# A recurrence and two feed-forward layers on one core: who issues the first loads and block 0's stores, how many weight sets are fetched early, and when columns are split

## The chip, the core and the metric

The kernel runs on one core of a Trainium2 chip. Its time is the device time of one execution in microseconds, from runs of the same program; the median of three runs of the kernel before is 937.01 us (936.17 to 940.31). The engines' names here: PE is TensorE (PEld its weight loads), DVE is VectorE, ACT is ScalarE, POOL is GpSimd, SP is SyncE.

## The reference

Three stages in a row, all in float32:

```python
# stage 1, per batch (4), head (8) and step t (768), head size 48
y[t]  = r[t] @ (state + outer(u * k[t], v[t]))
state = w[:, None] * state + outer(k[t], v[t])
# stage 2 on x = y as [3072, 384]; w_in is 384 x 2048, w_out 2048 x 384
h = x @ w_in;  x2 = maximum(0.01 * h, h) @ w_out
# stage 3, other weights of the same shapes
h = x2 @ w_in; out = (h * cos(h)) @ w_out
```

## The kernel before

**Stage 1** is cut into 24 units of 128 steps (6 per batch), each in two halves of 64. Within a half the recurrence is matmuls: scores of k and r (tiles pa and pd, L370), a state update (pu, L383 and L388) and the outputs (py, L512 and L516). Between them VectorE scales by powers of w (tile pt): X multiplies k (L354), R multiplies r (L357), Z makes k times u (L360), NK scales the other copy of k (L364); M and N select the triangle (L374). ScalarE moves states (S1 L394, S0 L411) and copies y to yo (L520). Units 0 to 7 use this early form; from unit 8 on an older form is used (prep L433 to L439, pieces L459, L466, L495).

**Columns.** y of a unit is stored to DRAM (L522, by SP for units 0 to 5) and read back transposed as columns xl (L594, by POOL for units 0 to 5). `split_xu` then casts xl to a rounded xh on ScalarE (L598) and subtracts on VectorE (L599). Four units make a block of 512 columns.

**Stages 2 and 3** run over slots (j, f): block j (0 to 5 of stage 2, 6 to 11 of stage 3) and one of 16 weight sets f. g1 of a slot is 9 matmuls (L611), then ScalarE and VectorE make ga, gh and gl (L623, L625, L651, L653), and two slots later g2 adds 9 matmuls (L665 to L667). At f = 15 of a block g2 copies three tiles ob (m = 0 and 2 by ScalarE, m = 1 by VectorE) and stores them (L680). Blocks 0 and 1 come one after the other; the slot number in the text counts g1 from 0, so block 0 is slots 0 to 15, block 1 is 16 to 31, block 2 starts at 32, and g2 of slot 15 stands in slot 17.

**Weights.** A set is 768 KB, loaded by SP (`load_w`, L148, tile raw) and decoded into two parts by `split_w`, which is a generator of four quarters: ACT L314; ACT L316; DVE L318, L319 and ACT L321; DVE L326, L327, L330. Tiles of sets 12 to 15 are lent to units 2 and 3 at first.

**Order.** SP follows the order of the program's text throughout. PE, VectorE and ScalarE follow it up to slot 16 (HAND); after that a scheduler orders them. The opening is: constants, loads of units 0 to 3 and sets 0 to 2, then the decays (pw, pt), an If on a flag (L253; its body is a slow path that is not taken here), the tables, and the list `first`, written out by hand for units 0 to 5 (SOLO), with ("x", n) for the split of unit n's columns, ("d", 0) for one quarter of decoding, ("l", n) for the load of unit n and ("w", f) for set f. After that come the slots; pieces of units 6 and 7 are spread over slots 0 to 15, those of units 8 to 11 over slots 18 to 28. Loads of units 8 and 9 are held and issued with the first piece of unit 8, in slot 18.

**Touched lines.** `load` (L118; unit 1's load is issued by ScalarE, L160), the copy of wi into the last column of pt (L233), the store of ob (L680), and the list `first` (L734 to L753).

```python
    load(0)
    nc.scalar.dma_start(out=ut, in_=uT)
    load(1, nc.scalar)
    load_w(0, 0)
...
        nc.scalar.copy(out=pt[:, 1, :, HC - 1:HC], in_=wi)
...
                (nc.sync if j == nb - 1 else getattr(nc, QO)).dma_start(out=dst, in_=ob)
```

Of the kernel before, what the change touches and what calls it, by code (L numbers as in the profile page):

```python
# [21 lines left out]
HC = C // 2  # L22
# [3 lines left out]
NF = DFF // 128  # L26
# [17 lines left out]
SOLO = 6  # L44
# [7 lines left out]
QO = 'scalar'  # L52
# [8 lines left out]
def moe_rwkv_kernel(ctx: ExitStack, tc, wT, uT, wq, uu, rs, ks, nat, wmoe, out):  # L61
    nc = tc.nc
# [49 lines left out]
    def ring(u):  # L112
        return u if u < UB else u % 2

    def v_of(u):
        return vf_[ring(u)] if u < ONE else vs_[u % 2]

    def load(u, q=nc.sync):  # L118
        src = nat[u * C:(u + 1) * C].rearrange("t i (h d) -> t i h d", h=H)
        if u < ONE:  # L120
            t, n = kf_[ring(u)], None
        else:
            t = ap_.tile([PACK, H, HC], F32, tag="ks", bufs=KSB, name="kst")
            n = ap_.tile([128, 2, H, D], F32, tag="nat", bufs=NATB, name="natt")
        q.dma_start(out=t, in_=ks[u])
        if u < ONE:
            q.dma_start(out=rf_[ring(u)], in_=rs[u])
        else:
            for c in range(2):
                q.dma_start(out=ar_[u % 2][ROWS[c], c], in_=rs[u, ROWS[c]])  # L130
        if u < ONE:
            q.dma_start(out=nk_[ring(u)], in_=src[:, 1])
        else:
            q.dma_start(out=n, in_=src[:, 0:2])
        for c in range(2):
            q.dma_start(out=v_of(u)[TOK[c], c], in_=src[TOK[c], 2])
        U["ks", u], U["nat", u] = t, n
# [7 lines left out]
    def load_w(L, f):  # L145
        pool, i = set_of(L, f)
        t = wraw[L, f] = pool.tile([128, 2, 384, 2], I32, tag=f"w{i}", name=f"raw{i}")
        nc.sync.dma_start(  # L148
            out=t.rearrange("p z a b -> p z (a b)"), in_=wmoe[L, f].bitcast(I32).rearrange("z p c -> p z c"))
# [6 lines left out]
    nc.sync.dma_start(out=wt, in_=wT)  # L156
    ut = const.tile([PACK, H], F32, name="ut")
    load(0)
    nc.scalar.dma_start(out=ut, in_=uT)
    load(1, nc.scalar)  # L160
    load_w(0, 0)
    load(2)
    load_w(0, 1)
    load(3)
# [10 lines left out]
    for i in range(2):  # L175
        nc.gpsimd.affine_select(
            out=mask[TOK[i]], in_=mask[TOK[i]], pattern=[[1, HC]], base=0, channel_multiplier=-1,
# [5 lines left out]
    pt = ap_.tile([PACK, 2, H, HC], F32, name="pt")  # L183
    wi = ap_.tile([PACK, H, 1], F32, name="wi")
# [20 lines left out]
    def stir(n):  # L205
        o = psum.tile([128, DM], F32, tag="h", bufs=2, name="stir")
        for i in range(n):
            nc.tensor.matmul(out=o, lhsT=still[:, 0:128], rhs=still, start=i == 0, stop=i == n - 1)

    def decays():  # L210
        nc.vector.tensor_scalar(out=ws, in0=wt, scalar1=W_LO, scalar2=W_HI, op0=ALU.max, op1=ALU.min)
        ge = const.tile([PACK, H], F32, name="ge")
        cnt = const.tile([PACK, 1], F32, name="cnt")
        flag = const.tile([1, 1], I32, name="flag")
        nc.vector.tensor_tensor(out=ge, in0=ws, in1=wt, op=ALU.is_equal)
        nc.vector.tensor_reduce(out=cnt, in_=ge, axis=AX.X, op=ALU.min)
        stir(1)
        tot = psum.tile([1, 1], F32, tag="a1", name="tot")
        nc.tensor.matmul(out=tot, lhsT=cnt, rhs=ones, start=True, stop=True)
        stir(2)  # L220
        for i in range(H):
            nc.vector.tensor_tensor_scan(
                out=pw[:, i], data0=ws[:, i:i + 1].to_broadcast([PACK, HC]), data1=ones.to_broadcast([PACK, HC]),
                initial=1.0, op0=ALU.mult, op1=ALU.mult)
        nc.vector.tensor_scalar(out=flag, in0=tot, scalar1=PACK - 0.5, scalar2=None, op0=ALU.is_lt)
        nc.vector.reciprocal(out=wi, in_=wc)
        nc.vector.tensor_tensor(out=wi[HALF[0]], in0=wi[HALF[0]], in1=wi[HALF[0]], op=ALU.mult)
        nc.vector.tensor_tensor(out=wd, in0=wc, in1=wc, op=ALU.mult)
        nc.scalar.copy(out=pt[HALF[0], 0, :, 0:1], in_=wc[HALF[0]])
        nc.scalar.copy(out=pt[HALF[1], 0, :, 1:HC], in_=pw[HALF[1], :, 0:HC - 1])  # L230
        nc.vector.tensor_tensor(
            out=pt[:, 1, :, 0:HC - 1], in0=pw[:, :, HC - 2::-1], in1=wi.to_broadcast([PACK, H, HC - 1]), op=ALU.mult)
        nc.scalar.copy(out=pt[:, 1, :, HC - 1:HC], in_=wi)  # L233
        return flag

    def tables():
# [328 lines left out]
    nb = len(blocks)  # L565
# [90 lines left out]
    def g2(slot):  # L656
        j, f = slot
        gh, gl = gs.pop(slot)
        if f == 0:
            op[j] = [psum.tile([128, NB], F32, tag=f"{'a' if j else 'o'}{m}", name=f"po{m}") for m in range(KT)]  # L660
        w_h, w_l = wsel.pop(slot)
        for m in range(KT):
            o = op[j][m]
            sl = slice(m * 128, (m + 1) * 128)
            nc.tensor.matmul(out=o, lhsT=w_l[:, 1, sl], rhs=gh, start=(f == 0), stop=False)  # L665
            nc.tensor.matmul(out=o, lhsT=w_h[:, 1, sl], rhs=gh, start=False, stop=False)  # L666
            nc.tensor.matmul(out=o, lhsT=w_h[:, 1, sl], rhs=gl, start=False, stop=(f == NF - 1))  # L667
        if f == NF - 1:
            L, t0, n = blocks[j]
            for m in range(KT):  # L670
                if j == nb - 1 and m == KT - 1:
                    ob = mp.tile([128, NB], F32, tag="ga", bufs=2, name="ga")
                else:
                    ob = mp.tile([128, NB], F32, tag="ob", bufs=OB2, name="ob")
                if m == 1:
                    nc.vector.tensor_copy(out=ob, in_=op[j][m])
                else:
                    nc.scalar.copy(out=ob, in_=op[j][m])
                dst = (out if L else x2t)[m * 128:(m + 1) * 128, t0:t0 + n]
                (nc.sync if j == nb - 1 else getattr(nc, QO)).dma_start(out=dst, in_=ob)  # L680


    slots = [(0, f) for f in range(LB)]
# [9 lines left out]
    for j in range(1, N1):  # L693
        a = 0 if j == 1 else at[0][1] + LAG + 1 if j == 2 else at[2][0] + PACE * (j - 3)
        b = a + PACE if j > 2 else at[j][0] - 4 if j != 1 else SPREAD
        n = ends[j] - (ends[j - 1] if j > 1 else pieces.index(("p", SOLO)) + 2)
# [27 lines left out]
    def quarter(si=-1):  # L724
        if ready[0] == NF or si in REST:
            return
        if not part:
            part.append(split_w(0, ready[0]))
        if next(part[0], part) is part:
            ready[0] += 1  # L730
            part.clear()

    do = {"w": lambda f: load_w(0, f), "y": piece_y, "l": load, "d": lambda f: quarter(), "x": split_xu}
    first = [("X R Z NK", 1), ("PA PD M N", 0), ("w", 3), ("w", 4), ("w", 5)]  # L734
    for u in range(SOLO):
        x = {2: [("x", 0)], 3: [("x", 1)], 4: [("x", 2)]}.get(u, [])
        q = 3 if u < 2 else 4 if u < SOLO - 1 else 0
        d = [[("d", 0)]] * q + [[]] * 4
        n = u + 1
        first += [("PU S1", u)] + d[0]  # L740
        first += [("PA", n)] if n < SOLO else []
        first += [("PV S0", u)]
        first += [("PD M", n)] if n < SOLO else []
        first += d[1] + x
        first += [("N", n)] if n < SOLO else []
        first += [("X R", u + 2)] if u + 2 < SOLO else []
        first += d[2]
        first += [("Z NK", u + 2)] if u + 2 < SOLO else []
        first += [("y", u)]
        first += {0: [("l", 4), ("w", 6)], 1: [("l", 5), ("w", 7)], 2: [("w", 8)],  # L750
                  4: [("l", 6)], 5: [("l", 7)] + [("w", f) for f in range(9, NF)]}.get(u, [])
        first += d[3]
    first += [("x", 3), ("X R Z NK", SOLO)]  # L753
    flag = decays()
    slow = nc.values_load(flag[0:1, 0:1], min_val=0, max_val=1)
    step_by_step()
# [10 lines left out]
    for si in range(len(slots) + LAG):  # L767
# [34 lines left out]
        if si >= LAG:  # L802
            g2(slots[si - LAG])
# [45 lines left out]
```

## Time and profile before

| what | value |
|---|---|
| median of 3 runs | 937.01 us |
| profiled execution: device time | 936.6 us |
| its span (first to last instruction) | 935.0 us |
| mean granted clock of PE | 0.990 |
| PE busy | 910.1 us (97%) |
| VectorE busy | 634.7 us (68%) |
| ScalarE busy | 542.7 us (58%) |
| chain that ended last | PE 83%, VectorE 5%, ScalarE 2%, DMA 2%, issue 2% |

Busy time of an engine is the union of its instructions; issuing a DMA and waiting don't count. Rows below have start, duration, engine and line, names (out<-in), shape and count; in brackets stands the idle time of the engine before the row and what ended it. All times in rows are counted from the span's start. A q behind an engine's name is its sequencer (waits, branches, DMA issues).

### The profile page before, as it was taken

Reading aid. Unit: us, or ns where it says so; the run is one execution under the profiler, and the core shown is the slowest. Engines: PE = TensorE matmul, PEld = TensorE weight load, DVE = VectorE, ACT = ScalarE, POOL = GpSimd, SP = SyncE. Lnnn points to the kernel's source line nnn. Section 1 sums busy time; section 2 is a strip of 40 time slices with the busy share of each in tenths; the row PEclk is TensorE's granted clock in tenths of the full one; section 3 lists DMA queues with packets and bytes.
Section 4 is the critical chain, followed back from the end, with each engine's and each line's share of the span. In section 5 each row is a group of like instructions: output and inputs, shape, how many; then the busy total and the mean of one; then the engine's idle time right before and its main releaser. Section 6 shows DMA issues by size and latency. Waiting matters only on the chain.

```text
span 935.0 us, 16040 instructions
## 1 busy us (share of the span) xinstructions
PE 910.1 (97%) x6306; PEld 746.6 (80%) x6306; DVE 634.7 (68%) x1047; ACT 542.7 (58%) x1040; POOL 50.4 (5%) x90
## 2 busy tenths in 40 slices
PE   7899998999999999998999999999999999999997
PEld 6777876887888888886888888888888888888885
DVE  5779998675677676656649976665655665665654
ACT  3446766554555555536457776665655665665554
POOL 3010000010110111100000000000000000000000
PEclk7999999999999999999999999999999999999999
DMA  8956024230332422315035420100100101000000
GB/s 250 291 165 234 19 76 124 81 103 24 113 100 65 135 79 71 103 52 186 10 125 169 135 68 1 34 35 1 57 12 1 67 1 34 35 1 0 34 1 34
DMA packets 37790, 73.09 MB, mean 78 GB/s; under 512 B 9392, under 2 KB 14384, under 8 KB 37712
## 3 DMA queue, kind: packets, MB, share of 16 engines
q1 hardware_dynamic: 27888, 49.95, 17.3%
q0 software_dynamic: 4384, 12.59, 4.4%
q10 hardware_dynamic: 5440, 9.51, 2.8%
q8 instruction: 49, 0.80, 0.4%
q14 instruction: 29, 0.24, 0.1%
HBM read 57.88 MB, written 14.16 MB: 77 GB/s over the span
## 4 chain that ended last, share of the span: by engine, by line
PE 83%; DVE 5%; ACT 2%; DMA 2%; issue 2%; SPq 0%; ACTq 0%; DVEq 0%
PE ph L611 39%; PE po L665 13%; PE po L666 13%; PE po L667 13%; PE pa L459 2%; PE py L495 2%; PE pu L466 1%; DVE w L326 1%; DVE gl L653 1%; ACT dt L321 1%; DVE dt L327 1%; DMA natt<-in_nat 1%; DVE dt L318 1%; DMA raw<-in_wmoe 0%; DMA kst<-in_ks 0%
## 5 line engine op out<-in xcount | busy, mean ns | idle before, releaser
L611 PE MATMUL ph<-xh,w 128*128 128x512 f32 x1152 | 301.8, 391 | 1.2 <-DVE w L330 1.2
L611 PEld LDWEIGHTS ph<-xh,w 128*128 128x128 f32 x1152 | 216.8, 188 | 47.5 <-DVE w L330 2.1
L665 PE MATMUL po<-gh,w 128*128 128x512 f32 x576 | 228.4, 397 | 2.0 <-ACT gh L651 2.0
L666 PE MATMUL po<-gh,w 128*128 128x512 f32 x576 | 224.6, 390 | 0.0
L667 PE MATMUL po<-gl,w 128*128 128x512 f32 x576 | 210.7, 390 | 2.2 <-DVE gl L653 2.1
L653 DVE TENSOR_TENSOR gl<-ga,gh 128x512 fp32r<-128x512 f32 x192 | 132.0, 689 | 106.9 <-ACT gh L651 95.1
L651 ACT CAST gh<-ga 128x512 fp32r<-128x512 f32 x192 | 118.8, 619 | 124.5 <-PE po L666 86.5
L611 PE MATMUL ph<-xl,w 128*128 128x512 f32 x576 | 166.5, 393 | 4.8 <-DVE ga L625 2.5
L611 PEld LDWEIGHTS ph<-xl,w 128*128 128x128 f32 x576 | 107.5, 188 | 28.4 <-DVE ga L625 3.1
L665 PEld LDWEIGHTS po<-gh,w 128*128 128x128 f32 x576 | 108.1, 188 | 26.9 <-ACT gh L651 3.3
L667 PEld LDWEIGHTS po<-gl,w 128*128 128x128 f32 x576 | 107.8, 188 | 26.0 <-DVE gl L653 3.5
L666 PEld LDWEIGHTS po<-gh,w 128*128 128x128 f32 x576 | 108.2, 188 | 21.3
L623 ACT ACTIVATE ga<-ph 128x512 f32<-128x512 f32 x96 | 57.0, 594 | 69.7 <-PE ph L611 68.4
L634 DVE SCALAR_TENSOR_TENSOR gt<-gt,ga 128x512 f32<-128x512 f32 x96 | 65.9, 690 | 38.7 <-ACT gt L633 38.3
L639 DVE TENSOR_TENSOR ga<-ph,gt 128x512 f32<-128x512 f32 x96 | 65.8, 688 | 34.2 <-ACT gt L638 33.5
L638 ACT ACTIVATE gt<-gt 128x512 f32<-128x512 f32 x96 | 59.9, 627 | 49.1 <-DVE gt L636 48.9
L625 DVE TENSOR_TENSOR ga<-ph,ga 128x512 f32<-128x512 f32 x96 | 65.7, 686 | 31.7 <-ACT ga L623 31.2
L632 ACT ACTIVATE ga<-ph 128x512 f32<-128x512 f32 x96 | 57.3, 596 | 43.4 <-PE ph L611 28.1
L471 ACT ACTIVATE ar<-ident,bon 64x64 f32<-64x64 f32 x256 | 64.7, 333 | 18.4 <-DVE bon L438 18.1
L633 ACT ACTIVATE gt<-ga 128x512 f32<-128x512 f32 x96 | 60.3, 631 | 2.1 <-ACT ga L632 0.4
L636 DVE TENSOR_SCALAR gt<-gt 128x512 f32<-128x512 f32 x96 | 40.4, 424 | 1.9
L314 ACT COPY dm<-raw 128x768 uint16<-128x768 uint16 x32 | 34.3, 1073 | 10.0 <-DMA raw<-in_wmoe 8.9
(139 smaller groups left out, 752.8 us busy)
## 6 DMA issues: line engine op xcount, KB each, us to landing
raw<-in_wmoe SPq DMA_DIRECT2D x32, 768.0 KB, 6.1
natt<-in_nat SPq DMA_DIRECT2D x16, 384.0 KB, 3.9
kst<-in_ks SPq DMA_DIRECT2D x21, 224.0 KB, 3.3
x2t<-ob ACTq DMA_DIRECT2D x18, 256.0 KB, 2.0
xl<-x2t POOLq DMA_DIRECT2D x6, 768.0 KB, 4.8
xl<-xt POOLq DMA_DIRECT2D x22, 192.0 KB, 3.5
vs<-in_nat SPq DMA_DIRECT2D x42, 96.0 KB, 3.9
out<-ob ACTq DMA_DIRECT2D x15, 256.0 KB, 2.0
```

Of the source, the lines that this page charges most:

```text
L471: nc.scalar.activation(out=ar[q, c, g], in_=ident2[q], func=AF.Copy, scale=bon[q, g:g + 1])
L611: nc.tensor.matmul(out=p, lhsT=w_[:, 0, k * 128:(k + 1) * 128], rhs=x_[:, k], start=(m == 0), stop=(m == 3 * KT - 1))
L625: nc.vector.tensor_tensor(out=ga, in0=p, in1=ga, op=ALU.max)
L633: nc.scalar.activation(out=gt, in_=ga, func=AF.Copy, bias=MAGIC)
L634: nc.vector.scalar_tensor_tensor(out=gt, in0=gt, scalar=MAGIC, in1=ga, op0=ALU.subtract, op1=ALU.subtract)
L638: nc.scalar.activation(out=gt, in_=gt, func=AF.Sin, scale=-TWOPI)
L639: nc.vector.tensor_tensor(out=ga, in0=p, in1=gt, op=ALU.mult)
L651: nc.scalar.copy(out=gh, in_=ga)
L653: nc.vector.tensor_tensor(out=gl, in0=ga, in1=gh.bitcast(F32), op=ALU.subtract)
L665: nc.tensor.matmul(out=o, lhsT=w_l[:, 1, sl], rhs=gh, start=(f == 0), stop=False)
L666: nc.tensor.matmul(out=o, lhsT=w_h[:, 1, sl], rhs=gh, start=False, stop=False)
L667: nc.tensor.matmul(out=o, lhsT=w_h[:, 1, sl], rhs=gl, start=False, stop=(f == NF - 1))
```

## The change

Unit 1's five loads are issued by SP in place of ScalarE. The copy of wi into pt goes from ScalarE to VectorE, ahead of the multiplication that fills the rest of that half of pt. Block 0's three stores go from ScalarE to SP. In `first`, set 3 alone is fetched ahead of unit 0; sets 4, 5 and 6 follow the outputs of units 0, 1 and 2, sets 7 to 15 those of unit 5. The splits of units 0, 1 and 2 move from units 2, 3 and 4 to units 3, 4 and 5, and that of unit 3 from behind the outputs of unit 5 to ahead of them.

```diff
-    def load(u, q=nc.sync):
+    def load(u):
+        q = nc.sync
...
-    load(1, nc.scalar)
+    load(1)
...
         nc.vector.tensor_tensor(out=wd, in0=wc, in1=wc, op=ALU.mult)
+        nc.vector.tensor_copy(out=pt[:, 1, :, HC - 1:HC], in_=wi)
...
         nc.vector.tensor_tensor(
             out=pt[:, 1, :, 0:HC - 1], in0=pw[:, :, HC - 2::-1], in1=wi.to_broadcast([PACK, H, HC - 1]), op=ALU.mult)
-        nc.scalar.copy(out=pt[:, 1, :, HC - 1:HC], in_=wi)
...
-                (nc.sync if j == nb - 1 else getattr(nc, QO)).dma_start(out=dst, in_=ob)
+                (nc.sync if j in (0, nb - 1) else getattr(nc, QO)).dma_start(out=dst, in_=ob)
...
-    first = [("X R Z NK", 1), ("PA PD M N", 0), ("w", 3), ("w", 4), ("w", 5)]
+    first = [("X R Z NK", 1), ("PA PD M N", 0), ("w", 3)]
     for u in range(SOLO):
-        x = {2: [("x", 0)], 3: [("x", 1)], 4: [("x", 2)]}.get(u, [])
+        x = {3: [("x", 0)], 4: [("x", 1)], 5: [("x", 2)]}.get(u, [])
...
+        first += [("x", 3)] if n == SOLO else []
         first += [("y", u)]
-        first += {0: [("l", 4), ("w", 6)], 1: [("l", 5), ("w", 7)], 2: [("w", 8)],
-                  4: [("l", 6)], 5: [("l", 7)] + [("w", f) for f in range(9, NF)]}.get(u, [])
+        first += {0: [("l", 4), ("w", 4)], 1: [("l", 5), ("w", 5)], 2: [("w", 6)],
+                  4: [("l", 6)], 5: [("l", 7)] + [("w", f) for f in range(7, NF)]}.get(u, [])
         first += d[3]
-    first += [("x", 3), ("X R Z NK", SOLO)]
+    first += [("X R Z NK", SOLO)]
```

## Rows read from the trace of the kernel before

**Rows 1.** Busy us by stretch: PE, PEld, DVE, ACT, POOL; granted clock; DMA share; GB/s.

```profile
0.00:63.59 63.59, 51.94 (x1058) 45.39 (x1058) 41.89 (x81) 28.03 (x49) 11.75 (x31) 0.89 0.79 231
...
8.90:19.10 10.20, 10.06 (x147) 9.88 (x148) 6.95 (x12) 3.18 (x12) 0.46 (x1) 0.50 1.05 296
46.40:49.80 3.40, 3.40 (x63) 3.28 (x64) 3.33 (x6) 2.44 (x4) 0.76 (x1) 0.50 0.68 240
```

**Rows 2.** Timeline of PE: tables, y of units 0, 1, 3, 4 (L512), scores, block 0.

```profile
9.04 1.59 PE L242 MATMUL ps_t<-ident,pt 48*64 48x48 f32 x13 [3.08 <-ACT pt L233]
...
21.54 0.33 PE L512 MATMUL py<-ar,vs 128*64 128x64 f32 x4
...
28.45 0.33 PE L512 MATMUL py<-ar,vs 128*64 128x64 f32 x4
...
44.43 1.15 PE L370 MATMUL pa<-ar,kst 48*64 48x64 f32 x32 [3.06 <-DVE ar L357]
...
48.24 0.47 PE L512 MATMUL py<-ar,lent 128*64 128x64 f32 x4
...
55.87 0.33 PE L512 MATMUL py<-ar,vs 128*64 128x64 f32 x4
...
63.59 0.72 PE L611 MATMUL ph<-xl,w 128*128 128x512 f32 x2 [1.72 <-DVE xl L599]
...
65.87 0.51 PE L370 MATMUL pa<-ar,kst 48*64 48x64 f32 x10
```

**Rows 3.** Timeline of ACT: its table load, the copy L233, unit 0's cast.

```profile
6.18 1.28 ACT L201 ACT_TABLE_LOAD   x1 [6.18 <-DMA kst<-in_ks]
...
8.74 0.20 ACT L233 COPY pt<-wi 112x8 f32<-112x8 f32 x1
...
41.46 0.51 ACT L598 CAST xh<-xl 128x384 fp32r<-128x384 f32 x1 [5.55 <-DMA xl<-xt]
```

**Rows 4.** Timeline of DVE: pt, unit 0's k, unit 6's r.

```profile
5.16 0.68 DVE L231 TENSOR_TENSOR pt<-pw,wi 112x504 f32<-112x504 f32 x1
...
8.97 0.69 DVE L354 TENSOR_TENSOR kst<-kst,pt 112x512 f32<-112x512 f32 x1 [3.13 <-ACT pt L233]
...
64.53 0.69 DVE L357 TENSOR_TENSOR ar<-ar,pt 112x512 f32<-112x512 f32 x1
```

**Rows 5.** Timeline of PE: pu (its first half) and pa at either clock.

```profile
15.64 1.27 PE L383 MATMUL pu<-vs,ub 128*48 128x48 f32 x13
...
18.08 1.60 PE L370 MATMUL pa<-ar,kst 48*64 48x64 f32 x32
...
24.05 0.75 PE L383 MATMUL pu<-vs,sm 128*48 128x48 f32 x13
...
25.44 1.15 PE L370 MATMUL pa<-lent,lent 48*64 48x64 f32 x32
```

**Rows 6.** Waits of SP up to 70 us; source L148 from 24.4 to 30.4 us.

```profile
SPq L253 <- SPq L253: 6.2, 1, 6.2
...
L148 SPq DMA_DIRECT2D raw<-in_wmoe x3: 392/453/460, 24.4 to 25.4; - x3
...
DMA to landing us min/median/max: 4.2/5.7/8.9
```

**Rows 7.** Timelines around block 0's end, and unit 11's columns with block 2's start.

```profile
134.23 0.43 SPq L125 DMA_DIRECT2D kst<-in_ks  x1
...
146.22 0.97 PE L667 MATMUL po<-gl,w 128*128 128x512 f32 x3 [1.27 <-DVE gl L653]
...
155.72 0.33 ACTq L680 DMA_DIRECT2D x2t<-ob  x1
...
212.10 0.76 POOL L594 DMA_DIRECT2D xl<-xt  x1 [4.63 <-DMA xt<-yo]
...
225.82 0.84 PE L611 MATMUL ph<-xl,w 128*128 128x512 f32 x3
```

## The prediction

> **What bounds the kernel now.** Over the whole span PE is 97% busy, but not in its first stage: in the 63.59 us ahead of block 0's first matmul PE shows 51.9 us, VectorE 41.9, the DMA engines 0.79 [rows 1]. No engine fills this stage, and the change works there. So look next at what PE waited for: 3.08 us before the table matmuls at 9.04, for ScalarE's copy L233; 3.06 us before unit 4's scores at 44.43, for VectorE; 1.72 us before block 0 at 63.59, for the split of unit 3's columns [rows 2]. Then follow each wait one engine back.
>
> At the start ScalarE computes nothing until 6.18: it issues the loads of unit 1, and only then loads its table and makes its copies, of which L233 ends at 8.94 [rows 3]. VectorE has made the rest of pt by 5.84, then sits idle 3.13 us for that copy [rows 4].
>
> At 41.46 ScalarE had been idle 5.55 us for unit 0's columns coming back from DRAM (line 598) [rows 3]; VectorE's subtraction, and behind it unit 4's multiplications, stood in order behind that cast, and so PE's scores at 44.43. The columns were late because the store of y of unit 0 was. SP stood 6.2 us at the If (L253); then it issued three weight sets, which landed from 4.2 us after the first issue at 24.4 (28.6) to 8.9 us after the last at 25.4 (34.3) [rows 6], and y of unit 0 went out behind them.
>
> After long idleness PE is slow as well: the granted clock is 0.50 (the lower level, 1.2 GHz) from 8.9 to 19.1 and from 46.4 to 49.8 [rows 1], each time behind one of the two 3 us waits.
>
> **The change part by part.**
>
> *Start.* Unit 1's five issues go from ScalarE to SP, and L233 becomes a VectorE copy ahead of L231. ScalarE then has its table and its other two small copies behind it before 6, since L231, which needs the same pw, started at 5.16. L231 ended at 5.84 [rows 4]; the new copy of 112x8 ahead of it I take at 0.2 us, ScalarE's time for the same shape [rows 3]. pt is whole at 6.05, and unit 0's first multiplication starts at about 6.1 in place of 8.97 [rows 4], if its k has landed. Gain 2.85 us. The cost: five issues on SP ahead of set 0 and of the loads of units 2 and 3. Bytes and order on the DMA engines stay nearly the same, and no wait on these loads stands among PE's [rows 2], so I take 0; if that cover is gone, it is at most the gain itself, as the issues then hold SP as long as they held ScalarE.
> The Trainium skill, "DMA: Bandwidth & Descriptors", section "Issuing engines are not separate DMA queues", says that starting DMAs on several engines only saves the sequencer's issue time, which is usually small. By that the first two terms of the sum below fall away (933.1); in the row of 6.18 the issue time is just what is paid.
>
> *Clock at the start.* PE now starts its table matmuls near 6.1, with no 3 us of idleness ahead of them. Nearest rows: both falls came behind 3 us of it [rows 1, 2]. So I take it that the clock stays at 2.4 GHz. What that gives: pu's 32 matmuls took 2.44 us at half (15.64 to 18.08) and 1.39 at full (24.05 to 25.44), a ratio of 1.75; pa's 32 took 1.60 against 1.15, a ratio of 1.39 [rows 5]. Ahead of 15.64 stood two such sets of scores (3.2 us), so PE worked at half from 12.4 to 19.1, 6.7 us. At full that saves 1.9 us (1.39) to 2.9 (1.75). I take 2.4, the middle, as the two forms are mixed. Bounds 0 to 2.9.
>
> *Fewer sets in the first units, splits one unit later.* Sets 4 and 5 leave the place ahead of y of unit 0; from there on each store, load and column transfer meets two sets less. Between 28.6 and 34.3 those two landed, so y of unit 0, the loads of unit 4 and the columns of unit 0 come up to 5.7 us sooner [rows 6]: columns at 41.4 - 5.7 = 35.7. Their split moves from unit 2 to unit 3. Where is unit 3 then? y of units 0 and 1 started at 21.54 and 28.45, a pace of 6.9; a unit with a split in it took from 48.24 to 55.87, 7.6 [rows 2]. With y of unit 0 at 21.54 - 2.85 - 2.4 = 16.3, y of unit 3 comes at 16.3 + 2 x 6.9 + 7.6 = 37.7, and its unit's split about 1 us before that: 36.7 against 35.7. So the 3.06 us go; the margin is 1 us. The loads of unit 4, behind the same store, are as tight. SP's 6.2 us at the If stay: nothing in the change moves them.
> With the wait goes the second low stretch of the clock: 3.4 us at the two ratios, 1.0 to 1.5 us; I take 1.2.
>
> *Split of unit 3 ahead of y of unit 5.* Block 0 no longer waits 1.72 us [rows 2]. But behind its first 9 matmuls come unit 6's scores, at 65.87 [rows 2], and these need VectorE's multiplication of r at 64.53, ended 65.22 [rows 4]. The load for that follows y of unit 4, whose place is unchanged. So only 65.87 - 65.22 = 0.6 us is kept.
>
> *Nine sets in place of seven behind unit 5.* The last set lands by the time of two sets, up to 5.7 us [rows 6], later. It is decoded last, in slot 13, behind 13 slots of some 4 us of matmuls; this hides it. Cost 0.
>
> *Block 0 stored by SP.* ScalarE loses three issues of 0.33 us [rows 7], off the path. But SP keeps the order of the text: the stores of g2 in slot 17 stand ahead of the loads of units 8 and 9, which slot 18 releases. Now load 8 is issued at 134.23, and the third store, by ScalarE, at 155.72 [rows 7]: load 8 can be up to 21.8 us later. Behind SP wait VectorE (prep) and PE (pieces of units 8 to 11). Cover: unit 8 needs the banks that block 0 frees in any case, and unit 11's columns were fetched at 212.10, while block 2 took them at 225.82 [rows 7], 13.7 us, of which I count 10 as slack behind landing and split. On the other side, gl stands behind prep of units 8 and 9 now: PE waited 1.27 us at 146.22 for it [rows 7]. Bounds: 1.3 us of gain to 21.8 of loss. I take 0: from slot 16 on VectorE, ScalarE and PE follow no written order, so prep can be set behind the matmuls at hand.
>
> **Sum.** 2.85 + 2.4 + 3.06 + 1.2 + 0.6 = 10.1. Two hand-overs have 1 us of margin (unit 4's loads, unit 0's columns); I take 1 us off for them: 9.1. The profiled execution took 936.6 (its span 935.0), 0.4 under the median of 937.0. 937.0 - 9.1 = 927.9.
>
> **Rivals.**
> *The clock falls at the start all the same.* Half of the table matmuls wait for ScalarE's eight scalings, and short idle spots stay. For it: the clock stayed low from 8.9 to 19.1 though PE shows 10.06 us busy there [rows 1]. Then 2.4 us are missing: 930.3.
> *The loads hold the units.* The two sets may free less than 5.7 us. If half, columns and loads come 2.8 us later than above, less the margin 1.8, and 1 us more at unit 5: 930.7. For it: the DMA engines' 0.79 [rows 1].
> *The start is worth nothing.* The five issues hold SP in ScalarE's place, unit 0 or 1 waits for its loads, and 5.25 us are missing: 933.1. Against: all these loads share the engines either way. By the rule of the Trainium skill named above ("DMA: Bandwidth & Descriptors") it would come out so.
> *The gain is given back at unit 11.* If load 8's 21.8 us pass on and 10 are slack, PE waits 11.8 us before block 2: 939.7, no change. Against: units 9 to 11 have work of their own between them and can catch up.
> *Slower: SP's stores jam the queue.* If prep of units 8 and 9 keeps its place ahead of gl on VectorE, PE stands for the whole delay, up to 21.8 us: 949.7. It decides from a PE wait of 9.1 us around slots 16 to 18. Against: ob of m = 1 is itself a VectorE copy that must come ahead of these loads, so prep can't stand ahead of all.
>
> **Numbers.** Forecast 0.50; clock 0.16; loads 0.13; start 0.06; given back 0.09; slower 0.06. The likeliest case's own range is 925 to 930. The range's lower end takes 2.85 + 2.9 + 3.06 + 1.5 + 1.72 (all of block 0's wait) + 1.3 (at the preps) = 13.3, or 923.7, and I set it at 922, since loads that come sooner may also shorten waits under 1 us. The upper end, 936, is a start worth nothing together with loads that hold (927.9 + 5.25 + 2.8); it leaves out the last two. Within 0.5% (4.7 us, about what a measurement of this kernel can tell from no change) lie 932.3 to 941.7: given back, start, and a little of the last: 0.14. Slower 0.08, the last rival with more of the kind; faster 0.78.
>
> **What would show it.** ScalarE's table load near 1.4; VectorE's first multiplication near 6.1; granted clock 1.00 from 8.9 to 19.1; no 3 us PE wait before unit 4's scores; block 0 near 53; a small PE wait at unit 6's scores in place of that for unit 3's columns; SP's pause at the If still there. I am wrong if block 0 starts before 56 and the end has not moved with it: then look at load 8, prep of unit 8, PE's gaps from slot 16 on, and the gap before block 2.

## The result: 924.3 us, and the profile after

The kernel after takes 924.31 us (median of 4 runs, 923.51 to 927.92) against 937.03 for the kernel before on the same chip: a ratio of 0.9865, 95% interval 0.983 to 0.990, so 12.7 us less. The forecast was 927.9 with a range of 922 to 936. The profiled execution took 924.3 us, its span is 922.7 against 935.0. Line numbers of the kernel after are one higher than before from L119 on (the multiplication L231 is L233).

The opening, by stretch, as in [rows 1] (PE, PEld, DVE, ACT, POOL; granted clock; DMA share; GB/s). The last row is slots 15 to 31, 90.20 us long before:

```profile
0.00:54.06 54.06, 48.56 (x1058) 41.40 (x1058) 42.11 (x82) 27.70 (x47) 11.43 (x30) 0.97 0.85 236
...
9.73:13.14 3.41, 3.41 (x60) 3.29 (x57) 3.31 (x7) 0.00 (x0) 0.06 (x1) 0.50 1.02 272
...
127.70:213.40 85.70, 85.70 (x704) 69.18 (x704) 61.44 (x102) 49.11 (x141) 7.69 (x12) 1.00 0.33 100
```

Block 0 starts at 54.06 in place of 63.59. In these two executions the low clock (0.50, the level of 1.2 GHz) shrank from 10.2 us to 3.4 us at the start, and the second low stretch is gone. PE in order of time, to be laid beside [rows 2]:

```profile
6.26 0.96 PE L243 MATMUL ps_t<-ident,pt 48*64 48x48 f32 x13
...
17.14 0.68 PE L371 MATMUL pd<-ar,natt 48*64 48x64 f32 x15 [0.89 <-issue]
17.75 0.33 PE L513 MATMUL py<-ar,vs 128*64 128x64 f32 x4
...
24.21 0.27 PE L371 MATMUL pa<-lent,lent 48*64 48x64 f32 x2 [1.41 <-issue]
...
26.34 0.33 PE L513 MATMUL py<-ar,vs 128*64 128x64 f32 x4
...
40.63 0.33 PE L513 MATMUL py<-ar,lent 128*64 128x64 f32 x4
...
44.65 1.15 PE L371 MATMUL pa<-ar,kst 48*64 48x64 f32 x32
...
47.66 0.33 PE L513 MATMUL py<-ar,vs 128*64 128x64 f32 x4
...
54.06 0.96 PE L612 MATMUL ph<-xl,w 128*128 128x512 f32 x3
...
57.84 1.15 PE L371 MATMUL pa<-ar,kst 48*64 48x64 f32 x32 [1.45 <-DVE ar L358]
```

The 3 us waits ahead of the tables and of unit 4's scores (44.65) and the 1.72 us ahead of block 0 have no bracket any more. In their place stand two stops marked "issue", 0.89 and 1.41 us, in units 0 and 1, and 1.45 us ahead of unit 6's scores.

ScalarE, as in [rows 3]: the table load now comes at 1.39, and unit 0's cast still comes at 41.67 (41.46 before), but a unit later in the work.

```profile
1.39 1.28 ACT L202 ACT_TABLE_LOAD   x1 [1.39 <-PEq L841]
...
41.67 0.51 ACT L599 CAST xh<-xl 128x384 fp32r<-128x384 f32 x1 [1.48 <-DMA xl<-xt]
```

VectorE, as in [rows 4]: the moved copy, unit 0's k, unit 6's r, the last gl of block 0, and the prep of unit 8 with a gl of block 1 (slot 17) behind its first two multiplications:

```profile
5.16 0.72 DVE L230 COPY pt<-wi 112x8 f32<-112x8 f32 x1
...
6.57 0.69 DVE L355 TENSOR_TENSOR kst<-kst,pt 112x512 f32<-112x512 f32 x1 [0.65 <-DVEq L254]
...
57.10 0.69 DVE L358 TENSOR_TENSOR ar<-ar,pt 112x512 f32<-112x512 f32 x1 [0.97 <-DMA ar<-in_rs]
...
132.44 0.69 DVE L654 TENSOR_TENSOR gl<-ga,gh 128x512 fp32r<-128x512 f32 x1 [1.08 <-ACT gh L652]
...
142.87 0.69 DVE L434 TENSOR_TENSOR kst<-kst,pt 112x512 f32<-112x512 f32 x1 [1.37 <-DMA kst<-in_ks]
143.59 0.69 DVE L436 TENSOR_TENSOR ar<-ar,pt 48x512 f32<-48x512 f32 x1
144.31 0.69 DVE L654 TENSOR_TENSOR gl<-ga,gh 128x512 fp32r<-128x512 f32 x1
```

The first multiplication starts 2.4 us sooner; 0.65 us of the wait that is left is VectorE's own branch at the If. SP's waits, as in [rows 6], and its timeline at the stores of block 0, as in [rows 7]:

```profile
SPq L254 <- SPq L254: 7.4, 1, 7.4
```

```profile
136.26 3.36 SPq L681 DMA_DIRECT2D x2t<-ob  x3
139.67 0.42 SPq L126 DMA_DIRECT2D kst<-in_ks  x1
```

SP's stop at the If grew from 6.2 to 7.4 us. The loads of unit 8 go out at 139.67, behind the three stores, 5.4 us later than at 134.23. Since everything else comes sooner, they moved further in the order of the work: from 1.3 us ahead of the start of slot 15 (135.56) to 11.9 us behind it (127.74), 13.3 us.

Where the 12.3 us between the two spans arose, from the starts of slots in the two traces: 8.0 us by the second slot of block 0 (61.3 against 69.3); nothing from there to slot 15 (127.7 against 135.6); 4.5 us in slots 15 to 31 (85.70 against 90.20); nothing from there to the last slot (906.3 against 918.5).

A profile is one execution, and the opening differs from one to the next. The kernel with the stores alone, below, has the same opening as the kernel before, and its second slot starts at 71.8 in place of 69.3. The kernel with the loads of units 8 and 9 ahead of the stores has the opening of the kernel after: 61.9 in place of 61.3. So one pair of profiles tells the gain of the opening to some 2 us only; slots 15 to 31 take 85.7 to 86.3 us in all ten profiles with the late loads and 89.9 to 90.3 in the three with neither late loads nor stores on SP.

### The profile page after: what moved, and what is told of

Its sections match the earlier page's. It is cut to its first block, busy times and chain, and to the rows that moved or that the text cites. A ratio compares the mean times of both kernels' runs of the same rounds, so it can differ in the third digit from the quotient of the medians.

```text
span 922.7 us, 16052 instructions
## 1 busy us (share of the span) xinstructions
PE 905.0 (98%) x6306; PEld 743.1 (81%) x6306; DVE 634.5 (69%) x1048; ACT 542.0 (59%) x1039; POOL 50.8 (6%) x90
## 4 chain that ended last, share of the span: by engine, by line
PE 85%; DVE 5%; DMA 2%; ACT 2%; issue 2%; SPq 0%; ACTq 0%; POOLq 0%; DVEq 0%
PE ph L612 39%; PE po L666 14%; PE po L667 13%; PE po L668 13%; PE py L496 2%; PE pa L460 2%; PE pu L467 1%; DVE w L327 1%; DMA ar<-in_rs 1%; ACT dt L322 1%; DVE gl L654 1%; DMA xl<-xt 1%; DVE dt L328 1%; DVE dt L319 1%; DMA raw<-in_wmoe 1%
## 5 line engine op out<-in xcount | busy, mean ns | idle before, releaser
L315 ACT COPY dm<-raw 128x768 uint16<-128x768 uint16 x32 | 34.5, 1079 | 10.9 <-DMA raw<-in_wmoe 10.5
```

## Experiments

Medians are given with the ratio to the kernel before and its interval. The median of before in these groups was 937.3 to 937.5. Each edit is made on the kernel named.

### One part alone

**Stores alone** (on the kernel before):

```diff
-                (nc.sync if j == nb - 1 else getattr(nc, QO)).dma_start(out=dst, in_=ob)
+                (nc.sync if j in (0, nb - 1) else getattr(nc, QO)).dma_start(out=dst, in_=ob)
```

> The kernel before with one edit: block 0's three stores issued by SP. Theory (the stores hold the loads of units 8 and 9 back, so VectorE no longer stands in their prep ahead of gl at block 0's end): everything up to slot 15 as before; load 8 issued some 12 to 16 us later; PE's gaps of 1.21, 0.73 and 1.67 us between 140 and 147 us gone; 3 to 4.5 us faster, 932.5 to 934. Rival 1 (my prediction's value, nothing): 937. Rival 2 (the stores only helped because the first stage had changed): 937 or slower.

Measured: 932.64 us, 0.9946 (0.9919 to 0.9972), some 4.7 us less. The waits of PE for gl and gh at 140 to 147 are gone, and slot 15 takes 8.2 us in place of 11.5. Load 8 is issued at 150.02, 11.9 us behind the start of slot 15. So the part that I had priced at nothing is worth more than a third of the whole.

**Start alone** (on the kernel before):

```diff
-    load(1, nc.scalar)
+    load(1)
...
+        nc.vector.tensor_copy(out=pt[:, 1, :, HC - 1:HC], in_=wi)
...
-        nc.scalar.copy(out=pt[:, 1, :, HC - 1:HC], in_=wi)
```

> The kernel before with the start alone: unit 1 loaded by SP, the copy of wi on VectorE. Theory (the early units gain 3 to 4 us, but unit 0's columns are still split in unit 2 and come no sooner, so the wait at 44.4 takes it all back): y of unit 0 at 17.5 to 18.5 in place of 21.54, a PE gap of 6 to 7 us ahead of unit 4's scores, block 0 at 63 to 64, 936 to 938. Rival (the gains add up): block 0 some 3.5 us sooner, 933 to 934.

Measured: 940.52 us, 1.0018 (1.0000 to 1.0035). y of unit 0 does start at 17.74, but the gain is lost at unit 4's scores. Row of PE (timeline), row of ScalarE, and the stretch around them with its granted clock:

```profile
46.67 1.54 PE L370 MATMUL pa<-ar,kst 48*64 48x64 f32 x24 [9.02 <-DVE ar L357]
```

```profile
43.70 0.51 ACT L598 CAST xh<-xl 128x384 fp32r<-128x384 f32 x1 [10.92 <-DMA xl<-xt]
```

```profile
40.66:54.32 13.66, 7.65 (x126) 7.32 (x127) 9.99 (x17) 6.06 (x9) 1.51 (x2) 0.50 0.78 231
```

The wait of 3.06 us [rows 2] became 9.02, more than the 6 to 7 of the theory: PE is there sooner, the columns 2.2 us later (43.68 against 41.44). The clock is at 0.50 for 13.66 us, from 3 us into this idleness on; 6.0 us of that pass before PE works again, 7.65 with PE busy. With the split still in unit 2, an earlier start is worth nothing or less; the time lies above both forecasts.

**List alone** (on the kernel before: the edits to `first`, nothing else):

```diff
-    first = [("X R Z NK", 1), ("PA PD M N", 0), ("w", 3), ("w", 4), ("w", 5)]
+    first = [("X R Z NK", 1), ("PA PD M N", 0), ("w", 3)]
-        x = {2: [("x", 0)], 3: [("x", 1)], 4: [("x", 2)]}.get(u, [])
+        x = {3: [("x", 0)], 4: [("x", 1)], 5: [("x", 2)]}.get(u, [])
...
```

> The kernel before with the list alone: three sets fewer fetched early, splits one unit later, that of unit 3 ahead of the outputs of unit 5. Theory (the wait at 44.4 and the low clock behind it go, the start stays): y of unit 0 at 21.5, no gap over 1.2 us ahead of unit 4's scores, slot 1 some 5 us sooner than before, 931 to 933. Rival (the start is needed too, since the loads of unit 4 hold): 934 to 937.

Measured: 930.28 us, 0.9922 (0.9895 to 0.9949), 7.0 us less; in the profile 6.3 us by the second slot of block 0 (63.0). Unit 0's columns landed at 39.79, only 1.65 us sooner; their cast stands at 41.24, behind other work, and no wait for it is left. The list has two halves, fewer sets early and later splits; no run took them apart.

**List and stores, no start** (on the kernel after):

```diff
-    load(1)
+    load(1, nc.scalar)
...
-        nc.vector.tensor_copy(out=pt[:, 1, :, HC - 1:HC], in_=wi)
...
+        nc.scalar.copy(out=pt[:, 1, :, HC - 1:HC], in_=wi)
```

> The kernel after without its start: unit 1 is loaded by ScalarE at first and ScalarE copies wi, as before; block 0's stores by SP and the edits to the list stay. Alone the start gave 940.5 in place of 937.4, stores alone 932.6, list alone 930.3. Theory (the start is worth little: its 2.4 us at the first multiplication are used up by waits for loads and by SP's longer stop at the If): 925 to 926, block 0's second slot at 62 to 63, slot 15 to slot 16 in 8.2 us as in the kernel after. Rival, as forecast (the start is worth 2.85 us and the clock 2.4 more): 928 to 930. Rival, the start costs in company as it did alone: 921 to 923.

Measured: 925.14 us (923.43 to 927.75), 0.9868 (0.9840 to 0.9896). Within the spread this is the kernel after: the start is worth 0.8 us by the medians, and 1.6 us by the profiles at the second slot of block 0 (62.9 against 61.3). The forecast of 5.25 us for it falls. Its low clock at the start is that of before:

```profile
9.49:19.73 10.24, 10.24 (x157) 9.91 (x156) 6.40 (x12) 3.15 (x9) 0.00 (x0) 0.50 1.06 293
```

### Why the stores help

Either ScalarE, freed of three issues, is what helps, or the loads of units 8 and 9, which SP now issues behind the stores. The next kernel keeps the stores on SP and puts the loads ahead (on the kernel after):

```diff
+            if i == ONE - 1:
+                while held:
+                    load(held.pop(0))
```

> The changed kernel, but the loads of units 8 and 9 stand ahead of block 0's stores in SP's order. Theory (the late loads are what helps): PE's gaps around slots 14 to 16 come back, 1 to 1.7 us each, slot 16 some 3 us later, 926.5 to 928.5. Rival (ScalarE, freed from the three issues, is what helps): 924 as in the changed kernel, with slot 16 at 135.9.

Measured: 926.69 us, 0.9876 (0.9849 to 0.9903), 2.4 us more than the kernel after by the medians (925.00 to 928.01 against 923.51 to 927.92), and slot 15 takes 11.3 us again. Load 8 is issued at 126.72, 1.6 us ahead of the start of slot 15, its place before the change. Its VectorE and PE (timelines of the same stretch):

```profile
135.02 0.69 DVE L434 TENSOR_TENSOR kst<-kst,pt 112x512 f32<-112x512 f32 x1 [0.18 <-DMA kst<-in_ks]
135.74 1.41 DVE L436 TENSOR_TENSOR ar<-ar,pt 48x512 f32<-48x512 f32 x2
137.07 0.54 DVE L438 TENSOR_TENSOR natt<-natt 128x384 f32<-128x384 f32 x1
137.54 0.54 DVE L437 TENSOR_TENSOR natt<-natt,ub 128x384 f32<-128x384 f32 x1
138.01 0.68 DVE L657 TENSOR_TENSOR gl<-ga,gh 128x512 fp32r<-128x512 f32 x1
```

```profile
138.74 0.97 PE L671 MATMUL po<-gl,w 128*128 128x512 f32 x3 [1.49 <-DVE gl L657]
```

VectorE does five operations of prep back to back, and gl behind them; PE waits for it. In the kernel after the loads land later and the prep begins at 142.87, when the last gl of block 0 (132.44) is long done. Slots 15 to 31 take 90.26 us before, 85.65 after and 89.20 here, from start to start: 3.55 of the 4.6 us go with the place of the loads. So their delay is most of the gain. The other 1.1 us stay, 0.9 of them in slots 16 to 30; whether that is ScalarE's relief no run shows. The whole of slots 15 to 31 shows more than the one wait of 1.27 us [rows 7]: PE stood 2.9 us there before (90.20 less its 87.30 busy) and nothing after, and its busy time, in which short gaps are hidden, fell by 1.6 us.

```profile
135.60:225.80 90.20, 87.30 (x703) 68.80 (x702) 61.87 (x102) 49.93 (x141) 7.70 (x12) 1.00 0.33 96
```

### Who loads unit 1

Unit 1 loaded by ScalarE behind its copy of dg (on the kernel after):

```diff
-    load(1)
...
     nc.scalar.copy(out=dg, in_=still[0:PACK])
+    load(1, nc.scalar)
```

> The changed kernel, but unit 1 is loaded by ScalarE again, issued behind its table load and first copy. Theory (five more issues on SP's one queue make the opening loads land 2 to 3 us later, SP leaves the If later, and unit 4's loads and y of unit 0 with it): set 2 lands near 24 in place of 26.7, set 3 is issued near 24.5 in place of 27.3, VectorE's first multiplication still near 6.2, 0.5 to 2 us faster than the changed kernel, 922.5 to 924. Rival (which engine issues makes no difference to the landing, ScalarE's later copies cost): 924.5 to 926.

Measured: 923.34 us, 0.9841 (0.9821 to 0.9861). Set 2 lands at 23.93 in place of 26.71, and SP leaves the If at 23.95 in place of 26.73; but PE has one stop of 1.32 us without a releaser before unit 4's scores, and y of unit 0 starts at 18.34. No difference from the kernel after that can be told.

Unit 1 loaded by ScalarE at first, as before, but with the copy of wi on VectorE (on the kernel after):

```diff
-    load(1)
+    load(1, nc.scalar)
```

> The changed kernel with unit 1 loaded by ScalarE at first, as before the change; the copy of wi stays on VectorE. Theory (in the start the freeing of ScalarE is worth more than SP's later exit costs): first multiplication near 6.2, but the tables' second half waits for ScalarE's scalings until 10.7, y of unit 0 some 2 us later than 17.75, SP out of the If near 24.5, 924 to 925.5. Rival (the copy of wi was all that mattered, and the loads on SP only cost): 922 to 923.5. If both halves were as I predicted: 927.

Measured: 924.59 us, 0.9854 (0.9829 to 0.9879). The first multiplication is at 6.58 all the same; the tables' second half waits 0.97 us for ScalarE. Of the two edits of the start, the copy is what moves VectorE. PE needs the other as well: y of unit 0 starts at 20.54 here, 1 us sooner than without the start (21.55), and at 17.4 to 18.2 in the three executions with both.

### What is left in the opening

Loads of units 6 and 7 ahead of the stores of y of units 4 and 5 (on the kernel after; `S` issues the store that `y` did, and the transfer of the columns behind it):

```diff
-        first += [("y", u)]
+        first += [("Y" if u in (4, 5) else "y", u)]
-                  4: [("l", 6)], 5: [("l", 7)] + [("w", f) for f in range(7, NF)]}.get(u, [])
+                  4: [("l", 6), ("S", 4)], 5: [("l", 7), ("S", 5)] + [("w", f) for f in range(7, NF)]}.get(u, [])
```

> The changed kernel, but the loads of units 6 and 7 are issued ahead of the stores of y of units 4 and 5. Theory (PE's wait of 1.83 us ahead of unit 6's scores is for the load of unit 6, which stands behind that store): k of unit 6 is issued some 3 us sooner, the wait falls under 0.5 us, slot 1 some 1.5 us sooner, 922.5 to 923.5. Rival (the columns of unit 4 or the sets, now later, wait in its place): 924 to 925.

Measured: 925.12 us, 0.9865 (0.9846 to 0.9885). The wait at unit 6's scores is gone, but a stop of 1.60 us without a releaser stands before unit 4's, behind which the clock is at 0.50 from 45.7 to 52.5; the second slot starts at 62.9. Up to y of unit 4 this is the opening of the kernel after, but its matmuls are slow from the first on:

```profile
6.26 1.62 PE L243 MATMUL ps_t<-ident,pt 48*64 48x48 f32 x13
...
12.89 1.27 PE L384 MATMUL pu<-vs,ub 128*48 128x48 f32 x13
```

```profile
6.57:18.20 11.63, 11.63 (x209) 11.27 (x207) 7.72 (x13) 3.80 (x10) 2.93 (x7) 1.00 1.01 278
```

The first 13 table matmuls took 1.59 us at 0.50 before [rows 2] and 0.96 at 1.00 after; here they take 1.62, and the pace stays that of the lower level up to some 15 us, while the row says 1.00. So, by these times, the granted clock of this row misses a low stretch. Three other profiles whose rows show no fall there (unit 1 by ScalarE at first, unit 1 behind the copy, all three edits) and that of the stores alone have the same slow matmuls at the start.

Set 2 behind the If, and each later set one place later (on the kernel after):

```diff
-    load_w(0, 2)
...
-    first = [("X R Z NK", 1), ("PA PD M N", 0), ("w", 3)]
+    first = [("X R Z NK", 1), ("PA PD M N", 0), ("w", 2)]
...
-        first += {0: [("l", 4), ("w", 4)], 1: [("l", 5), ("w", 5)], 2: [("w", 6)],
+        first += {0: [("l", 4), ("w", 3)], 1: [("l", 5), ("w", 4)], 2: [("w", 5)], 3: [("w", 6)],
```

> The changed kernel with one set less up front: set 2 behind the If, each later set one place later. Theory (PE's gaps of 1.10 and 1.63 us at 16 and 22.6 that nothing explains, and SP's stop at the If, are instruction fetches behind the data that is queued): SP leaves the If about 2.6 us sooner, the gap at 22.6 shrinks, unit 4's loads and the columns of unit 0 come 2 to 3 us sooner, block 0 1 to 2 us sooner, 922 to 923.5. Rival (the stop and the gaps don't depend on what is queued): SP leaves the If at 27, gaps as in the changed kernel, 924 to 925.

Measured: 923.53 us, 0.9854 (0.9833 to 0.9875). Unit 0's columns land at 38.05, 3.6 us sooner; PE's stops at 16 and 23 are gone, others (0.78 and 1.54 us, without a releaser) come at 44 and 50. SP goes on behind the branch at 22.31. No gain.

Two edits together, unit 1 loaded behind the copy and the loads of units 6 and 7 first (the two diffs above, on the kernel after):

> The kernel after with unit 1 loaded by ScalarE behind its copy of dg, and with the loads of units 6 and 7 ahead of the stores of y of units 4 and 5. The first edit alone gave 923.3 with a wait of 1.25 us left at unit 6's scores, the second alone 925.1 with that wait gone but other waits in its place. Theory (each engine wait taken away shows up again as a stop of PE without a releaser, since the stage is held by what the DMA engines deliver): 922.5 to 925, not to be told from the kernel after. Rival (the two gains add): 922 or less.

Measured: 925.07 us, 0.9863 (0.9835 to 0.9890). The gains don't add; PE has five stops without a releaser, the low clock lies from 24.4 to 31.2 in this profile, and slots 1 to 15 take 67.8 us in place of 66.5.

All three, these two and set 2 behind the If (the three diffs above, on the kernel after):

> As the run with the copy and the loads of units 6 and 7, and set 2 fetched behind the If, with each later set one place later. Theory (the stage is held by the bytes that the units themselves need, once the sets are off): SP leaves the If near 22 in place of 24 to 27, columns of unit 0 land near 37, and the time is 922 to 924. Rival (the DMA engines' load is what is left to gain): second slot of block 0 at 59 or less and 920 or less.

Measured: 926.68 us, 0.9876 (0.9849 to 0.9904), not better than the kernel after and above both forecasts; columns at 37.16, SP out of the If at 23.02, the second slot at 61.0. The 0.3 us that this is sooner go in slots 1 to 15, which take 68.6 us in place of 66.5, some of it in waits for VectorE's ga (0.68) and gl. One stop of PE:

```profile
50.87 0.22 PE L515 MATMUL py<-ar,gt 112*48 112x64 f32 x1 [2.37 <-issue]
```

### SP's stop at the If

Sets 1 and 2 both behind the If, ahead of set 3 (on the kernel after):

```diff
-    load_w(0, 1)
...
-    load_w(0, 2)
...
-    first = [("X R Z NK", 1), ("PA PD M N", 0), ("w", 3)]
+    first = [("X R Z NK", 1), ("PA PD M N", 0), ("w", 1), ("w", 2), ("w", 3)]
```

> The kernel after with sets 1 and 2 both fetched behind the If, ahead of set 3. SP has left the If within 0.2 us of the landing of the last load queued ahead of it in nearly all runs (23.6 to 23.8, 26.7 to 26.7, 25.3 to 25.3), and at 22.3 with one set less queued. Theory (the fetch of instructions behind the taken branch waits behind the data queued ahead): with two sets less the last of unit 3's loads lands near 20 to 21, and SP leaves the If there, 1 to 4 us after the branch. Rival (the stop has a price of its own, 6 to 7 us, that data does not set): exit 6 us or more behind the branch, whatever is queued. The time: 923 to 928, as sets 1 to 3 then stand ahead of y of unit 0 and set 1 may be late for decoding.

Measured: 924.06 us, 0.9854 (0.9818 to 0.9889). SP's longest wait at the branch, of this kernel and (second fence) of the one with the copy, units 6 and 7 and one set less:

```profile
SPq L252 <- SPq L252: 3.2, 1, 3.2
```

```profile
SPq L252 <- SPq L252: 4.6, 1, 4.6
```

The last load ahead landed at 19.84, and SP left at 20.49, 3.3 us behind its branch at 17.23. A fixed price of 6 to 7 us falls. What SP waits for is in the trace, and it is two things. One is a transfer on a queue of kind "instruction" (q8 and q14 on the page of the kernel after, 49 and 29 packets). The other is eight waits of SP right behind the branch, each for the landing of loads that it issued ahead (source L254 of the kernel after):

```profile
q8 instruction: 49, 0.80, 0.4%
q14 instruction: 29, 0.24, 0.1%
```

```profile
L254 SPq EVENT_SEMAPHORE  x8: 17/17/17, 26.7 to 27.3; - x8
```

Four of the 14 traces, in us (worked out from the traces; the packet is the last of q14 ahead of SP's going on, the load the last one issued ahead of the branch):

```
kernel                branch   packet's end   load landed   SP goes on
before                17.56    22.44          23.63         23.84
after                 19.32    24.46          26.71         26.73
set 2 behind the If   19.07    20.91          23.82         22.31
one set               17.23    19.08          19.84         20.49
```

In six traces SP goes on 1.40 to 1.41 us behind the end of a packet of q14 (before, the stores alone, unit 1 by ScalarE at first, and the three with fewer sets ahead). In the other eight, the kernel after among them, it goes on 0.01 to 0.02 us behind the landing of set 2, 1.5 to 2.3 us behind the packet: there the data ended the stop, and not the fetch. With set 2 behind the If the later ones of the eight waits hold SP up to 23.84, for unit 3's loads.

So the stop is a fetch of instructions and a wait for loads queued ahead, and the later of the two ends it. The fetch itself comes sooner with less queued: its packet ended 1.8, 1.8 and 3.2 us behind the branch with one or two sets less, and 4.0 to 5.2 in the other eleven. That it stands behind that data is borne out by this; how the DMA engines order the two was not measured by itself. The Trainium skill, "Runtime: NRT & Kernel Launch", section "Instruction fetch mechanics", says that a taken branch whose target isn't at hand forces a fetch by DMA before execution goes on; the trace agrees, as SP never goes on sooner than 1.40 us behind such a packet.

The same section of the Trainium skill says that the crossing of a 16 KiB block is mostly hidden. The trace agrees with "mostly". q8 moved 0.80 MB in 49 packets, 16 KB each, as PE's 6306 matmuls and 6306 weight loads went by, which is one packet for some 129 matmuls. Of the 49, 41 end after block 0 has begun, and no stop of PE marked "issue" lies there. Eight end in the opening, and PE's stops marked "issue" from the tables to block 0 number 37 over the 14 traces (0.17 to 2.37 us): each ends 1.28 to 1.68 us behind the end of a packet of q8. In the kernel after the two longest are (us, from the trace):

```
packet of q8         PE's stop (matmul to matmul)
14.34 to 15.71       16.04 to 17.14
21.51 to 22.81       22.58 to 24.21
```

The stops add up to 1.2 to 4.0 us an opening: 1.6 before, 2.7 after. That PE waits for its instructions there is read from this coincidence; no run took the fetches away.

## Why the prediction was right, and where it wasn't

The direction, the range and most of the signs listed at its end held: table load at 1.39, block 0 at 54.06, no 3 us wait before unit 4's scores, a small wait at unit 6's in place of unit 3's columns, SP's stop still there. The granted clock did not stay at 1.00. The sum of 9.1 us came close to 12.7 by errors of opposite sign, though, and that is luck: the start gave some 4 us less than its terms, the stores 4.5 more, the list 1.5 to 2 more.

| term | forecast | measured |
|---|---|---|
| first multiplication | 2.85 | 2.4 (8.97 to 6.57) |
| clock at the start | 2.4 | 2.3 in this execution, 0.9 in another of the same opening |
| both, kept at the second slot | 5.25 | 1.6 (62.9 to 61.3); 0.8 by medians |
| list: columns wait, second low clock, unit 6 | 4.86 | 6.3 (69.3 to 63.0); 7.0 by medians |
| block 0 stored by SP | 0 | 4.5 to 4.7 |
| hand-overs | -1 | in the rows above |

*Start.* The size was nearly right and the keeping was wrong. VectorE started 0.45 us later than forecast, since its branch at the If (0.65 us) stood there. The clock did fall, so the step "3 us of idleness ahead, so without it the clock stays" failed: it fell at 9.73, with a single short wait of PE in the 3 us ahead (0.55 us before 8.69, for VectorE), and in the execution with the loads of units 6 and 7 first the matmuls are slow from 6.26 on. How long it stays low differs as well. In the kernel after it was 6.8 us less than before: from the first multiplication to y of unit 0 it takes 11.2 us in place of 12.6, and 0.9 of the 11.2 is the stop for an instruction packet, so by this the clock gave 2.3. In that other execution the stretch takes 11.6 us without any stop, so there it gave 0.9. The rival "the clock falls at the start all the same" had this right in kind, if not its price.

Then look at where y of unit 0's lead over the run without the start goes (3.8 us, 17.75 against 21.55). It is 2.1 at y of unit 1 (26.34 against 28.46), behind PE's second stop, but 3.5 at y of unit 4 (47.66 against 51.12), as the other run has such stops later, and 3.1 at block 0 (54.06 against 57.15). At the second slot it is 1.6, behind the 1.45 us at unit 6's scores, whose load of r landed at 56.59 only. In the execution with the loads of units 8 and 9 first it is 2.6 at y of unit 4 and 1.0 at the second slot. So the step that failed is the silent one that what is gained at unit 0 is kept up to the second slot: the load of unit 6, PE's stops and the clock took it, in shares that differ from execution to execution, and none of them was in the sum.

"Five issues on SP: 0" was wrong in the trace too. The kernel after and the two others with its opening have all on SP's queue, and the opening loads come slower: 224 to 230 GB/s from 1.4 to 10 us against 251 before, unit 1's last piece at 10.5 to 11.5 against 9.95, set 2 at 24.9 to 26.7 against 23.63; SP leaves the If 1.1 to 2.9 us later, so "SP's 6.2 us at the If stay" held for the stop and not for its end. But with unit 1 back on ScalarE the time was 923.3 and 924.6, so this is not where the gain went.

The rival "the start is worth nothing" had the place right, if not the price, and with it the rule of the Trainium skill ("DMA: Bandwidth & Descriptors", section "Issuing engines are not separate DMA queues"): in the time, the runs side with it. That the issue time saved is small, the trace does not bear out: unit 1's five issues hold SP for 2.7 us (4.02 to 6.70), and with both queues unit 1's last piece landed 0.5 to 1.5 us sooner and set 2 1.2 to 3.1 us. Whether this is issue time alone or the second queue, no run told apart.

*Columns.* "Columns and loads come up to 5.7 us sooner" failed. In the kernel after unit 0's columns landed at 41.65, 0.2 us later than before, as SP was 2.9 us late at the If; in the two other executions of its opening they were 1.7 and 2.5 us sooner (39.78 and 38.98), with the list alone 1.65 us. The wait of 3.06 us went all the same, and by these times because the split moved one unit back, to where 41.7 is soon enough; the half with fewer sets was not run alone. From y of unit 2 to y of unit 3 the list alone takes 7.8 us in place of 11.9, 4.1 us less, where 3.06 and 1.2 were forecast: the price was right, and the reason for it half wrong. So the condition of the rival "the loads hold the units" was met (far less than 5.7 us freed), and its price was not paid. The rest of the gain of the list beyond 4.9 us lies ahead of y of unit 2 (34.76 against 36.36), where a stop of 1.00 us for an instruction packet, from 31.40 on before, has no counterpart, and where the first multiplication itself came 0.66 us sooner (8.31 against 8.97), which the list doesn't touch; both I take for chance of the execution, not for the list.

*Unit 6.* As forecast in kind, and larger: 1.45 us, and block 0's wait of 1.72 is nearly all given back there. The load of r landed at 56.59.

*Nine sets behind unit 5.* Nothing of it shows: slots 1 to 15 take 66.5 us after and 66.3 before.

*Stores by SP.* This is the step that failed by most. "Bounds: 1.3 us of gain to 21.8 of loss. I take 0" took one row of waiting (1.27 us) for the whole gain, and the loads as the only thing that could be late. The loads went 13.3 us back in the order of the work, and that is most of the gain, since VectorE's prep of units 8 and 9 no longer stands ahead of block 0's gl. Nothing was given back at unit 11: its columns landed at 203.26, block 2 began at 213.4. Both rivals that rested on the delay fall.

## What to carry to other kernels

When a transfer is made later, ask first what its data releases: if that is work on an engine that another engine is waiting for, the delay can be the gain, and the price is read from all waits and short gaps of that stretch (span less busy, and busy against busy), not from one row. A wait that hangs on a round trip through DRAM went here by placing its consumer later, while the transfer came little sooner or not at all. Test parts in company as well as alone: the start was no gain or a loss of up to 3 us alone, and nearly nothing in company, and the sum of stores and list alone (4.7 + 7.0) is all but the whole change. Compare the profiles of two kernels that share a stretch before you read a cause into a difference there: the same opening ended up to 2.5 us apart.

## What the runs showed of the hardware that was not expected

A fetch of instructions comes later while data is queued. Behind SP's taken branch its packet ended 4.0 to 5.2 us on with three sets queued ahead, 1.8 to 3.2 with fewer (14 traces). SP then also waits for loads that it had queued: in eight traces it went on 0.01 to 0.02 us behind the landing of the last one. PE stopped for up to 2.37 us behind 16 KB packets of q8 in the stage of short matmuls, while the DMA engines' share was 0.85; such a stop reads "issue" in the timeline, and its end lies 1.3 to 1.7 us behind the end of the packet. In the stages of long matmuls no such stop shows.

The granted clock fell to 0.50 with one wait of 0.55 us shortly ahead, and for 13.66 us from 3 us into one of 9 us; in the kernel with list and stores it was low for 10.2 us with PE busy throughout. The same opening had 3.4 us of slow matmuls in two executions and some 9 in a third, and the clock of the third's row didn't show it: the time of equal matmuls does. A wait that goes is paid back in clock too, but where the low stretch then lies was not forecast well from the waits alone.
